# Attention with a routed expert layer: landmark inverse per two batches in two PSUM banks, q, k and v loads issued by ScalarE, and a new order of work

## The chip, the cores and the metric

The kernel runs on one core of a Trainium2 chip. The metric is the device time of one execution in microseconds (us); a kernel is run several times and the median counts. Engines are called PE (matrix products), VectorE (DVE in the profile), ScalarE (ACT), GpSimd (POOL) and SyncE (SP, which only issues DMAs here).

## The reference

Two layers follow each other. The first is a landmark attention over 8 batches x 8 heads, 576 rows of 64 values each; the second sends each of the 4608 rows (512 values) to one of 8 experts.

```
q_lm, k_lm = means of q and k over 18 rows each          # 32 landmarks per head
A  = softmax(q  k_lm^T / 8);  Bm = softmax(q_lm k_lm^T / 8);  C = softmax(q_lm k^T / 8)
Z  = Bm^T / (norm_1(Bm) * norm_inf(Bm) + 1e-6)
for _ in range(6): Z = 2 Z - Z Bm Z                       # approximate inverse of Bm
x  = A Z C v                                              # rows of all heads side by side
e  = argmax(x w_gate);  g = softmax(x w_gate)[e];  s = sigmoid((x w_output_gate)[e])
out = g * s * relu(x w1[e]) w2[e]
```

## The kernel before

Work is cut into 16 groups: a group is 4 heads of one batch, so that 4 x 32 landmarks fill the 128 partitions; two groups are a batch, two batches a pair. For each group q, k and v are loaded into a scratch region (`load`, L211 to L222; the region lies where the weights of the last three experts come later). GpSimd adds up the landmark sums of q and k (`landmark_sums`, L224, five additions each), ScalarE scales them (L239), PE transposes q, k and the landmarks in blocks that ScalarE copies out of PSUM (`transposes`, L243 to L258). PE then makes the scores C and A (L265) and Bm (a block of its own, L280). `softmax_c` (L268) reads C in a column order that the matmul's moving operand gives it, transposes the result (L298) and multiplies it with v (L308). `softmax_a` (L315) is VectorE work apart from one exponential; its result AT stays in SBUF.

`iteration(b)` (L340) serves one batch. With W = Z0 Bm scaled and V = Z0 C v kept side by side (96 columns), each of six steps applies W to both, and VectorE writes 2 cur - W cur (L379). Per step there are 2 groups x 4 heads = 8 matmuls of 32 x 32 x 96, on the four diagonal 32 x 32 tiles of the array, into one PSUM bank (`ps_m`). Column sums come from matmuls with a block of ones (L364). The end transposes V (L386), multiplies it with the gate weights (L397) and writes both masked by head into vbd (L391, L399).

`outputs(b)` (L406) makes five blocks of x per batch, four of 128 rows and one of 64 (L422); ScalarE casts x into a row tile (L426), VectorE adds up the gate logits (L428). `routing` (L448) serves a pair: argmax, place of each row in its expert's list, matmuls for the running counts (L499 to L501), then per block of 128 rows a GpSimd copy that puts row number and coefficient behind the row (L528) and a scatter into a DRAM list sorted by expert (L530).

The expert layer works on tiles of 128 rows of one expert: `fetch` (L670) reads rows and coefficients (SP), `turn_x` transposes them, `up` (L701) multiplies by w1 and ScalarE applies relu, `turn_h` transposes where needed, `down` (L732) multiplies by w2, VectorE scales (L743) and GpSimd scatters the result (L745). Weights are loaded by GpSimd with a cast (L142, L145), four parts per expert, the first experts once the first pair is ranked, the last three after the scratch region is free. Tiles come in stages: 8 and 10 tiles on the two fullest experts after the first pairs, 8 more, and a last stage that needs the last routing (L720 with operand x; here 12 tiles).

Order: each piece of work is a Python generator that issues instructions and yields: L loads, G landmark sums, M landmark scaling, T transposes, C and A the softmaxes, N the inverse, O outputs, R routing, E expert weights, X expert tiles. The string ORDER (L20) says which generator goes on next, so it fixes the order of instructions on every engine's queue; `need` (L187) holds a generator until a mark is set, and "want"/"hold" keep two users of one PSUM tile apart. Each engine runs its queue strictly in the order written, SP's loads included. PSUM has eight banks: `ps_m` 1, `ps_o` 2, `ps_t` 2, `ps_v` 1, and `ps_s` 2, which later serve the expert tiles.

Of the kernel before, what the change touches and what calls it, by code (L numbers as in the profile page):

```python
# [20 lines left out]
    "TTTGTTLTMCTGCTTACGCMCATTCTLMATCCTLAAAAGTCALCMTTCTCNGANLMCNATCGTLALCAACTGMCLTTANTLAMNCCTLGCANCNNLTCAN"  # L21
    "AANMGTCCTNNLTATAOLGAMCCNLGATOAACCTMAGNOCANTLTACTMNTANCLMNONNCACNLACNGOTTCGTMCANOALONTTATLOCCNOATNCGA"
    "AMNOCTRRCTCNARLRMNRTTTRLARCLNTNGCMNRRLGRRCRARAAACTCNCLTRTNLRNTAGOTLMATNRTEENRCRCONRCRNAGCNONTAMAACCG"
    "AEOTXTATNONLXCAALNCMGATTACCOTCAEAEXXOMXCOOLXTNMATXGAOLLRTRTNXERGLAXCXXMTXCNTRGCACRMTECCTAATNRARXMNCC"
    "XNXXNARRLTCENTAXCEXNXLTACTXLGTXARAALNLRGRETXXCNXMTNGCNAAXXONRXETXCNXNXAOLXANAOTNRAXNACOMNCGXTONCEXML"
    "TNALCRTXAGOCCXLXOTXXAMCXCAXGRETOCAOXXRCOTNNTTTXXERNXERCMNXXRRXXANREETXEXCNXRXARCRNXRRAXEMXEXREAETXXT"
    "CTXNXTRNRCTXRNXXXCLXAXEXCCEXXXXCRNCOXCEAAOAXXACXXXXXNEAXXAXXEXNOEXXEONXXNXXEOANRXXXXRXXNXXXRENXNXANE"
    "XXXXAXNXXXNAXXOXOOXOXXXOXRRRRRXRXXXXRXXRXXXXRRXXXRRRXXXXXXXXXRRXXXXXXRXXXXXXXRRXXXXXXXXXXXX"
# [4 lines left out]
def kernel(  # L33
# [14 lines left out]
    m = 32  # L48
# [54 lines left out]
    wg = cpool.tile([D, H, 2 * E], F32, name="wg")  # L103
# [56 lines left out]
    zeros = cpool.tile([128, ROW], I32, name="zeros")  # L160
    nc.vector.memset(zeros, 0)
    nc.vector.memset(zeros[:, HD // 2:HD // 2 + 1], 1 << 20)
# [15 lines left out]
    rows_p = ctx.enter_context(tc.tile_pool(name="rows", bufs=12))  # L178
# [24 lines left out]
    ps_v = ctx.enter_context(tc.tile_pool(name="ps_v", bufs=1, space=PSUM))  # L203
# [7 lines left out]
    def load(k, nm):  # L211
        b, gi = k // NG, k % NG
        src = dict(q=q, k=k_in, v=v)[nm][b, gi * HG:(gi + 1) * HG]
        if nm == "v":
            at = v_places[k % 2]
            t = tail[:CP, at:at + HG * C6 * D].rearrange("p (h x) -> p h x", h=HG)
            nc.sync.dma_start(out=t, in_=src.rearrange("h (p c) d -> p h (c d)", c=C6))
        else:
            at = qk_places[(2 * k + (nm == "k")) % 4]
            t = tail[:, at:at + g * D].rearrange("p (g d) -> p g d", d=D)  # L220
            nc.sync.dma_start(out=t, in_=src.rearrange("h (m g) d -> (h m) g d", g=g))
        groups[k][nm] = t  # L222

    def landmark_sums(k, nm):  # L224
# [4 lines left out]
        nc.gpsimd.tensor_tensor(s, t[:, :hg, :], t[:, hg:, :], op=OP.add)  # L229
        nc.gpsimd.tensor_tensor(s[:, 0:4, :], s[:, 0:4, :], s[:, 4:8, :], op=OP.add)  # L230
        nc.gpsimd.tensor_tensor(s[:, 0:2, :], s[:, 0:2, :], s[:, 2:4, :], op=OP.add)
        nc.gpsimd.tensor_tensor(s[:, 0:1, :], s[:, 0:1, :], s[:, 1:2, :], op=OP.add)
        nc.gpsimd.tensor_tensor(s1, s[:, 0:1, :], s[:, 8:9, :], op=OP.add)
        G["s" + nm] = s1
# [8 lines left out]
    def transposes(k):  # L243

        G = groups[k]
        for nm in ("q", "k"):
            tv = G[nm].rearrange("p (gp par) d -> p gp (par d)", par=2)
            lm = G["l" + nm].rearrange("p a d -> p (a d)")
# [3 lines left out]
            for c0 in range(0, hg + 1, 4):  # L252
                n = min(4, hg + 1 - c0)
                p = ps_t.tile([128, 4, 128], F32, tag="tp", name="tp")
# [5 lines left out]
    def scores(p, lhs, rhs, cols=lambda x: x):  # L260
        for par in range(2):
            pr = slice(64 * par, 64 * par + 64)
            for h in range(HG):
                hs = slice(32 * h, 32 * h + 32)
                nc.tensor.matmul(p[hs, par, :hg * 32], lhsT=lhs[pr, hg, hs], rhs=cols(rhs[pr, :hg, hs]))  # L265
        return p[:, :, :hg * 32]

    def softmax_c(k):  # L268
        G = groups[k]
        b, gi = k // NG, k % NG  # L270
        if gi == 0:
            batches[b]["BC"] = sm.tile([128, NG, 32 + D], F32, tag="BC", name="BC")
        BC = batches[b]["BC"]

        p = ps_s.tile([128, 2, 512], F32, tag="S", name="S")
        sC = scores(p, G["qT"], G["kT"], lambda x: x.rearrange("p (g3 c2) m -> p c2 m g3", g3=CG))
        sC = sC.rearrange("p par (c2 x) -> p par c2 x", x=CP)
        for h in range(HG):
            hs = slice(32 * h, 32 * h + 32)
            nc.tensor.matmul(p[hs, 0, hg * 32:hg * 32 + 32], lhsT=G["qT"][0:64, hg, hs],  # L280
                             rhs=G["kT"][0:64, hg, hs])
        mark("scored C", k)
        nm = sm.tile([128, 1], F32, tag="nm", name="nm")
        nc.vector.tensor_reduce(nm, sC, axis=AX.XYZ, op=OP.max, negate=True)
        yield "hold", "s"
        rc = sm.tile([128, 1], F32, tag="rc", name="rc")
        eC = se.tile([128, g, 32], F32, tag="eC", bufs=1, name="eC")
        nc.scalar.activation(out=eC.rearrange("p g m -> p (g m)").rearrange("p (c2 par x) -> p par c2 x", par=2, x=CP),
                             in_=sC, func=EXP, bias=nm, accum_out=rc)
# [4 lines left out]
        by_chunk = eC.rearrange("p (c x) m -> p c (x m)", c=C6)  # L294
        for c0 in range(0, C6, 3):
            p = ps_t.tile([128, 4, 128], F32, tag="tp", name="tp")
            for c in range(c0, c0 + 3):
                nc.tensor.transpose(p[:CP, c - c0, :], in_=by_chunk[:, c], identity=I128)  # L298
# [3 lines left out]
        yield "want", "v"  # L302
        pv = ps_v.tile([128, 128], F32, tag="pv", name="pv")[:, :D]
# [7 lines left out]
        yield "hold", "v"  # L311
# [3 lines left out]
    def softmax_a(k):  # L315
# [19 lines left out]
        AT = sb.tile([128, g * 32], F32, tag="AT", bufs=6, name="AT")  # L335
        nc.vector.transpose(out=AT, in_=At.rearrange("p a b -> p (a b)"))
        batches[k // NG].setdefault("AT", []).append(AT)
        mark("soft", k)

    def iteration(b):  # L340
        BC = batches[b]["BC"]

        mB = sm.tile([128, NG], F32, tag="mB", name="mB")
# [8 lines left out]


        def apply_w(cur, lo):
            p = ps_m.tile([128, NG, 32 + D + 32], F32, tag="m", name="pw")
            for gi in range(NG):
                for h in range(HG):
                    hs = slice(32 * h, 32 * h + 32)
                    nc.tensor.matmul(p[hs, gi, lo:32 + D], lhsT=cur[hs, gi, :32], rhs=cur[hs, gi, lo:])  # L359
            return p  # L360

        p = apply_w(BC, 0)
        for gi in range(NG):
            nc.tensor.matmul(p[:, gi, 32 + D:], lhsT=blk, rhs=BC[:, gi, :32])  # L364
        ci = sm.tile([128, NG], F32, tag="ci", name="ci")
        nc.vector.tensor_reduce(ci, p[:, :, 32 + D:], axis=AX.X, op=OP.max)
        nc.vector.tensor_scalar(out=ci, in0=ci, scalar1=1e-6, scalar2=None, op0=OP.add)
        nc.vector.reciprocal(ci, ci)
        cur = sm.tile([128, NG, 32 + D], F32, tag="WV", name="WV")
        nc.vector.tensor_tensor(cur, p[:, :, :32 + D], bc(ci, 32 + D), op=OP.mult)  # L370
        yield
        for it in range(6):
            lo = 0 if it < 5 else 32
            p = apply_w(cur, lo)
            if it < 5:
                nxt = sm.tile([128, NG, 32 + D], F32, tag="WV", name="WV")
            else:
                nxt = sm.tile([128, NG, D], F32, tag="V", name="V")
            nc.vector.scalar_tensor_tensor(out=nxt, in0=cur[:, :, lo:], scalar=2.0,  # L379
                                           in1=p[:, :, lo:32 + D], op0=OP.mult, op1=OP.subtract)  # L380
            cur = nxt
            yield

        pt = ps_m.tile([D, NG, 128], F32, tag="m", name="pt")
        for gi in range(NG):
            nc.tensor.transpose(pt[:, gi, :], in_=cur[:, gi, :], identity=I128)  # L386
        VT = sm.tile([D, NG, 128], F32, tag="VT", bufs=1, name="VT")
        nc.scalar.copy(VT, pt)
        vbd = sm.tile([128, NG, 2, VC], F32, tag="vbd", name="vbd")
# [3 lines left out]
        pg = ps_m.tile([128, NG, 2 * E], F32, tag="m", name="pg")  # L393
        for gi in range(NG):
            for h in range(HG):
                hs = slice(32 * h, 32 * h + 32)
                nc.tensor.matmul(pg[hs, gi, :], lhsT=VT[:, gi, hs], rhs=wg[:, gi * HG + h, :])  # L397
        for h2 in range(2):
            nc.scalar.activation(out=vbd[:, :, h2, D:], in_=pg, func=COPY, scale=hm[:, h2:h2 + 1])  # L399
        batches[b]["vbd"] = vbd  # L400
        mark("vbd", b)
        yield

    def outputs(b):

        pair, bb = b // 2, b % 2  # L406
        P = pairs[pair]
        if bb == 0:
            P["L"] = sm.tile([128, CPP, 2 * E], F32, tag="L", name="L")
            P["rows"] = [None] * CPP  # L410
        L, rows = P["L"], P["rows"]
        vbd, ATs = batches[b]["vbd"], batches[b]["AT"]
        for c in range(5):
            t, n, p0 = (4 * bb + c, 128, 0) if c < 4 else (8, 64, 64 * bb)
            ps = slice(p0, p0 + n)
            if rows[t] is None:
                rows[t] = rows_p.tile([128, ROW], I32, tag="row", name="row")
            po = ps_o.tile([128, 2, 512], F32, tag="o", name="po")
            for gi in range(NG):
                for hp in range(2):  # L420
                    hs = slice(64 * hp, 64 * hp + 64)
                    nc.tensor.matmul(po[ps, hp, gi * 2 * VC:(gi + 1) * 2 * VC],  # L422
                                     lhsT=ATs[gi][hs, 128 * c:128 * c + n],
# [584 lines left out]
```

## Time and profile before

| | |
|---|---|
| median of 3 runs | 379.78 us (378.74 to 384.86) |
| profiled execution | 376.81 us |
| its span, first to last instruction | 375.2 us |
| mean granted PE clock | 0.985 of full speed |
| DMA traffic | 66.76 MB, 178 GB/s over the span |
| largest groups | L737 PE 73.9 us, L256 PE 51.2, L257 ScalarE 47.9, L229 GpSimd 43.0 |

How to read it: a row of a group view names line, engine, operation, output <- input and count, then the busy time in us and the mean ns of one, then the engine's idle time just before, and what ended it. A row of waits says who waited for whom: us in total, times, longest. A row of a timeline has the start, the length, and in brackets the idle time before. Rows of busy time by stretch give each engine's busy us, then granted clock, DMA share and GB/s. An fp32 matmul leaves two records.

### The profile page before, as it was taken

How to read it: one execution, taken by the hardware profiler on the slowest of the kernel's cores; microseconds unless marked ns; L12 is line 12 of the kernel's file. 1: busy time of each engine (PE TensorE's matmuls, PEld its weight loads, DVE VectorE, ACT ScalarE, POOL GpSimd, SP SyncE). 2: the span in 40 equal slices, each digit the busy share in tenths (PEclk: the TensorE clock that was granted, in tenths of full speed). 3: DMA queues.
4: the chain of work that ended last, by engine and by line, in shares of the span. 5: the costliest groups of instructions: out<-in, count | busy, mean ns of one | idle time of the engine just before them, and what ended most of it. 6: DMA issues, size and time to landing. Idle time of an engine off the chain costs nothing. (4 is left out here: it accounts for less than half of the span.)

```text
span 375.2 us, 11946 instructions
## 1 busy us (share of the span) xinstructions
PE 323.5 (86%) x4532; PEld 208.1 (55%) x4532; DVE 221.2 (59%) x584; ACT 175.0 (47%) x413; POOL 215.5 (57%) x319
## 2 busy tenths in 40 slices
PE   2888879888888877999998899999979997899992
PEld 1555456565655645676666477666645553455551
DVE  6277677477977384777658672665635674223322
ACT  2676475766737553554555354543234331232320
POOL 3788855644887487278888465784420585122322
PEclk9999899999989998999999999999999999999999
DMA  8866555245637997895587799999992357354221
GB/s 254 268 192 207 176 190 168 71 145 190 184 145 139 293 261 156 216 236 202 116 243 190 146 243 255 228 229 247 228 259 89 117 180 172 64 91 121 73 86 50
DMA packets 46743, 66.76 MB, mean 178 GB/s; under 512 B 16208, under 2 KB 35024, under 8 KB 46672
## 3 DMA queue, kind: packets, MB, share of 16 engines
q0 software_dynamic: 17568, 31.24, 37.4%
q1 hardware_dynamic: 29104, 34.63, 31.9%
q8 instruction: 39, 0.64, 0.7%
q14 instruction: 32, 0.26, 0.3%
HBM read 65.35 MB, written 16.23 MB: 217 GB/s over the span
## 5 line engine op out<-in xcount | busy, mean ns | idle before, releaser
L745 POOL DMA_INDIRECT out_dram<-y,ic x38 | 39.1, 1030 | 88.1 <-DVE y L743 69.9
L737 PE MATMUL py<-W,hT 128*128 (+1 forms) x304 | 73.9, 382 | 6.9 <-DMA W<-in_moe_w_dram 4.0
L743 DVE TENSOR_SCALAR y<-py,ic 128x512 f32<-128x512 f32 x38 | 28.4, 749 | 60.2 <-PE py L737 59.9
L257 ACT COPY W<-tp 128x512 f32<-128x512 f32 (+1 forms) x96 | 47.9, 515 | 31.9 <-PE tp L256 31.6
L256 PE MATMUL tp<-ident,W 128*128 128x128 f32 x288 | 51.2, 298 | 13.3 <-ACT W L257 7.8
L229 POOL TENSOR_TENSOR lms<-W 128x576 f32<-128x576 f32 x30 | 43.0, 1435 | 31.6 <-DMA W<-in_q_dram 30.6
L737 PEld LDWEIGHTS <-hT 128*128 128x128 bf16 x304 | 29.1, 99 | 39.1 <-issue 6.6
L723 ACT ACTIVATE h<-ph 128x512 bf16<-128x512 f32 x40 | 23.9, 597 | 56.0 <-PE ph L720 51.2
L256 PEld LDWEIGHTS tp<-ident,W 128*128 128x128 f32 x288 | 34.5, 148 | 24.5 <-ACT W L257 12.3
L530 POOL DMA_INDIRECT x_sorted<-row,r_slot x36 | 36.7, 1020 | 13.5 <-POOL row L528 8.8
L709 PE MATMUL ph<-xT,W 128*128 128x128 bf16 x576 | 37.7, 219 | 1.5 <-DMA W<-in_moe_w_dram 0.7
L422 PE MATMUL po<-vbd,AT 64*128 64x160 f32 (+1 forms) x320 | 32.8, 324 | 4.4 <-DVE L L428 3.4
L709 PEld LDWEIGHTS <-W 128*128 128x128 bf16 x576 | 33.2, 98 | 4.8 <-issue 2.6
L428 DVE TENSOR_REDUCE L<-po 128x16 f32<-128x128 f32 (+1 forms) x40 | 11.6, 290 | 40.2 <-ACT row L426 40.2
L712 ACT ACTIVATE hT<-ph 128x512 bf16<-128x512 f32 x36 | 21.4, 597 | 27.8 <-PE ph L709 27.6
L426 ACT CAST row<-po 128x512 bf16<-128x512 f32 (+1 forms) x40 | 23.4, 585 | 21.1 <-PE po L422 17.6
L265 PE MATMUL S<-W 64*32 64x288 f32 x512 | 26.1, 466 | 5.7 <-ACT BC L290 4.1
L359 PE MATMUL pw<-WV 32*32 32x96 f32 (+1 forms) x768 | 25.6, 249 | 5.6 <-DVE WV L379 3.4
L422 PEld LDWEIGHTS po<-vbd,AT 64*128 64x128 f32 (+1 forms) x320 | 22.5, 178 | 11.8 <-DVE L L428 5.7
L230 POOL TENSOR_TENSOR lms<-lms 128x256 f32<-128x256 f32 x30 | 24.9, 830 | 2.4
L359 PEld LDWEIGHTS pw<-WV 32*32 32x32 f32 x768 | 15.5, 107 | 16.0 <-DVE WV L379 7.4
L720 PE MATMUL ph<-W,x 128*128 x96 | 22.7, 379 | 1.7 <-DMA out_dram<-y,ic 1.3
(166 smaller groups left out, 530.0 us busy)
## 6 DMA issues: line engine op xcount, KB each, us to landing
W<-in_moe_w_dram POOLq DMA_DIRECT2D x32, 512.0 KB, 11.2
W<-in_q_dram SPq DMA_DIRECT2D x16, 576.0 KB, 6.6
W<-in_k_dram SPq DMA_DIRECT2D x16, 576.0 KB, 6.7
W<-in_v_dram SPq DMA_DIRECT2D x16, 576.0 KB, 5.2
x<-x_sorted SPq DMA_DIRECT2D x26, 128.0 KB, 6.4
x_sorted<-zeros SPq DMA_DIRECT2D x9, 136.0 KB, 1.9
ic<-x_sorted SPq DMA_DIRECT2D x38, 1.0 KB, 5.5
out_dram<-y,ic POOLq DMA_INDIRECT x38, 2.9
```

The lines of the kernel that those rows point to most:

```text
L229: nc.gpsimd.tensor_tensor(s, t[:, :hg, :], t[:, hg:, :], op=OP.add)
L230: nc.gpsimd.tensor_tensor(s[:, 0:4, :], s[:, 0:4, :], s[:, 4:8, :], op=OP.add)
L256: nc.tensor.transpose(p[:, i, :], in_=tv[:, c0 + i] if c0 + i < hg else lm, identity=I128)
L257: nc.scalar.copy(tT[:, c0:c0 + n, :], p[:, :n, :])
L265: nc.tensor.matmul(p[hs, par, :hg * 32], lhsT=lhs[pr, hg, hs], rhs=cols(rhs[pr, :hg, hs]))
L359: nc.tensor.matmul(p[hs, gi, lo:32 + D], lhsT=cur[hs, gi, :32], rhs=cur[hs, gi, lo:])
L422: nc.tensor.matmul(po[ps, hp, gi * 2 * VC:(gi + 1) * 2 * VC], lhsT=ATs[gi][hs, 128 * c:128 * c + n], rhs=vbd[hs, gi].rearrange("p a b -> p ...
L530: i = nc.gpsimd.indirect_dma_start(out=xs, out_offset=bass.IndirectOffsetOnAxis(ap=slot[:, c:c + 1], axis=0), in_=rows[c], in_offset=None)
L709: nc.tensor.matmul(ph[:, 128 * i:128 * i + 128], lhsT=columns(t, dc * F + (half * FCH // 2 + i) * 128, 128), rhs=t["xT"][:, dc, :], start= ...
L737: nc.tensor.matmul(t["py"], lhsT=t["hT"][:, fc, :], rhs=columns(t, DCH * F + fc * HD, HD), start=(fc == 0), stop=(fc == FCH - 1))
L743: nc.vector.tensor_scalar(out=y, in0=t["py"], scalar1=t["coef"], scalar2=None, op0=OP.mult)
L745: i = nc.gpsimd.indirect_dma_start(out=out, out_offset=bass.IndirectOffsetOnAxis(ap=t["id"], axis=0), in_=y, in_offset=None, bounds_check= ...
```

## The change

- The inverse serves a pair (four groups) at once. The tile has two PSUM banks, one for each batch. The second batch's heads move between neighbouring tiles (head h sits in the partitions of h or of h^1, in turn), so that its matmuls run on off-diagonal tiles. VectorE writes S = 2I - W (a new function `complement`), which is the stationary operand, ScalarE copies the new W and V. Column sums take two matmuls per pair (one with a swapped block of ones). V is transposed for two groups in one go, and the gate weights lie block-wise on 128 partitions with zeros between, so one matmul per head and batch serves both groups.
- `scores` appends Bm as a tenth block of columns to C's first half; the column order that C needs is made by ScalarE when it applies the exponential. AT is written as 512 + 64 columns (AT, AU).
- `outputs` serves a pair: eight blocks of 128 rows and one that holds the two 64-row rests.
- From group 2 on, ScalarE issues the q, k and v loads. Group 0's landmark sums are the five additions, on VectorE.
- `ps_v` is gone: pv and the routing counts use `ps_t`. The routing writes one row block at a time; its coefficient is a VectorE reciprocal straight into the row tile, the row number a GpSimd copy made one block ahead. The end-of-list markers are copied from DRAM to DRAM.
- ORDER is a new string (another order of the same generators); y has three buffers instead of four.

```diff
-    def load(k, nm):
+    def load(k, nm, eng):
...
-            nc.sync.dma_start(out=t, in_=src.rearrange("h (m g) d -> (h m) g d", g=g))
+            eng.dma_start(out=t, in_=src.rearrange("h (m g) d -> (h m) g d", g=g))
...
-                load(k, nm)
+                load(k, nm, nc.scalar)
...
-    def scores(p, lhs, rhs, cols=lambda x: x):
+    def scores(p, lhs, rhs, more=0):
...
+            n = hg + more * (1 - par)
...
-                nc.tensor.matmul(p[hs, par, :hg * 32], lhsT=lhs[pr, hg, hs], rhs=cols(rhs[pr, :hg, hs]))
+                nc.tensor.matmul(p[hs, par, :n * 32], lhsT=lhs[pr, hg, hs], rhs=rhs[pr, :n, hs])
...
-        pv = ps_v.tile([128, 128], F32, tag="pv", name="pv")[:, :D]
+        pv = ps_t.tile([128, 512], F32, tag="tp", name="pv")[:, :D]
...
+        def apply_w(p, lhs, rhs, lo, swaps, swap):
             for gi in range(NG):
+                for bb in range(2):
+                    for h in range(HG):
+                        at = h ^ (bb & swaps)
+                        to = at ^ (bb & swap)
+                        hs, os = slice(32 * at, 32 * at + 32), slice(32 * to, 32 * to + 32)
+                        nc.tensor.matmul(p[os, NG * bb + gi, lo:32 + D], lhsT=lhs[hs, NG * bb + gi], rhs=rhs[hs, NG * bb + gi, lo:])
+
+        def complement(S, W):
+            nc.vector.scalar_tensor_tensor(out=S, in0=W, scalar=-1.0, in1=twice, op0=OP.mult, op1=OP.add)
...
         for it in range(6):
             lo = 0 if it < 5 else 32
-            p = apply_w(cur, lo)
+            p = banks()
+            apply_w(p, S, cur, lo, (it + 1) % 2, it < 5)
             if it < 5:
...
+                complement(S, p[:, :, :32])
+                nc.scalar.copy(cur, p[:, :, :32 + D])
             else:
...
-            nc.vector.scalar_tensor_tensor(out=nxt, in0=cur[:, :, lo:], scalar=2.0,
-                                           in1=p[:, :, lo:32 + D], op0=OP.mult, op1=OP.subtract)
...
+                nc.scalar.copy(cur, p[:, :, 32:32 + D])
...
+        for t in range(CPP):
+            if t == ROWS - CPP and pair >= 1:
+                yield from need("routed", pair - 1)
...
+        name_row(0)
         for c in range(CPP):
-            if c % 2 == 0:
-                yield
-            nc.gpsimd.tensor_copy(rows[c][:, HD // 2:].rearrange("p (n x) -> p n x", x=2),
-                                  idc[:, c, None, :].to_broadcast([128, META // 2, 2]))
+            yield
+            nc.vector.reciprocal(rows[c][:, HD // 2:HD // 2 + 1].bitcast(F32), co[:, c:c + 1])
             i = nc.gpsimd.indirect_dma_start(
...
+            if c + 1 < CPP:
+                name_row(c + 1)
```

More of the change, by code (lines that the diff above doesn't have):

```diff
@@ L407, in outputs @@
         P = pairs[pair]
[L408 to L417, printed above, removed]
-            po = ps_o.tile([128, 2, 512], F32, tag="o", name="po")
[L419 to L423, printed above, removed]
-                                     rhs=vbd[hs, gi].rearrange("p a b -> p (a b)"))
-            pv = po[ps, :, :NG * 2 * VC].rearrange("p t (gh e) -> p t gh e", e=VC)
-            nc.scalar.copy(rows[t].bitcast(BF16)[ps, :HD].rearrange("p (t gh d) -> p t gh d", t=2, d=D),
+        L = P["L"] = sm.tile([128, CPP, 2 * E], F32, tag="L", name="L")
@@ L806, in softening_a @@
             if k >= 6:
-                yield from need("out", (k - 6) // NG)
+                yield from need("half" if (k - 6) % (2 * NG) < NG else "out", (k - 6) // (2 * NG))
             yield from softmax_a(k)
```

264 lines of the change are left out of this document (148 added, 116 removed).

## The prediction, made before the changed kernel had run

> **What bounds the kernel now.** I read the page's busy line first, then the busy time by stretch, then the waits of PE, POOL and SP, and last the timelines around the places that the change touches.
>
> ```profile
> PE 323.5 (86%) x4532; PEld 208.1 (55%) x4532; DVE 221.2 (59%) x584; ACT 175.0 (47%) x413; POOL 215.5 (57%) x319
> ```
> ```profile
> core 0: us, PE busy (x) PEld busy (x) DVE busy (x) ACT busy (x) POOL busy (x), PEclk, DMA share, GB/s
> 20.00:105.00 85.00, 71.60 (x1385) 47.91 (x1385) 62.65 (x163) 54.55 (x146) 57.89 (x87) 0.98 0.56 176
> 105.00:150.00 45.00, 34.98 (x567) 24.06 (x560) 28.14 (x74) 24.03 (x59) 33.30 (x48) 0.92 0.81 191
> 150.00:290.00 140.00, 132.05 (x2001) 90.34 (x2001) 86.11 (x245) 65.97 (x153) 82.26 (x113) 1.00 0.93 210
> ```
> PE is the busiest engine everywhere. From 150 to 290 us it idles 8.0 of 140 us: work taken off PE there shortens the time one for one. From 20 to 105 us it idles 13.4 of 85 us and from 105 to 150 us 10.0 of 45 us, so other things share the limit. The waits say which:
>
> ```profile
> PE tp L256 <- ACT W L257: 7.8, 11, 2.9
> PE py L737 <- DMA W<-in_moe_w_dram: 4.0, 1, 4.0
> PE pw L359 <- DVE WV L379: 3.4, 8, 0.7
> ```
> ```profile
> POOL lms L229 <- DMA W<-in_q_dram: 30.6, 8, 6.5
> ```
> ```profile
> SPq L221 <- PE tp L256: 26.2, 11, 8.1
> ```
> PE waits for many short ScalarE copies and once, for 4.0 us, for weights. POOL waits 30.6 us for q and k loads, which feed its landmark sums and then PE. SP holds q and k loads back, 26.2 us in all, until PE has transposed the old tile, so they are just in time.
>
> **PE work that the change removes.** Start-to-start times of PE's timeline give the price of each block:
>
> ```profile
> 150.71 0.53 PE L359 MATMUL pw<-WV 32*32 32x96 f32 x16
> 151.17 0.21 PE L499 MATMUL pr<-r_ohb,neg_lower_bf 128*128 128x72 bf16 x1
> ```
> ```profile
> 162.08 0.71 PE L265 MATMUL S<-W 64*32 64x288 f32 x16
> 162.73 0.88 PE L308 MATMUL pv<-W 96*32 96x64 f32 x48
> 163.54 0.66 PE L256 MATMUL tp<-ident,W 128*128 128x128 f32 x4
> ```
> ```profile
> 167.87 0.32 PE L397 MATMUL pg<-wg,VT 64*32 64x16 f32 x16
> 168.12 0.40 PE L697 MATMUL pt<-ident_bf,x 128*128 128x128 bf16 x4
> ```
> ```profile
> 193.16 0.89 PE L265 MATMUL S<-W 64*32 64x288 f32 x16
> 193.83 0.25 PE L280 MATMUL S<-W 64*32 64x32 f32 x8
> 194.01 0.40 PE L697 MATMUL pt<-ident_bf,x 128*128 128x128 bf16 x4
> ```
> ```profile
> 205.72 0.76 PE L422 MATMUL po<-vbd,AT 64*64 64x160 f32 x8
> 206.41 0.33 PE L256 MATMUL tp<-ident,W 128*128 128x128 f32 x1
> ```
> ```profile
> 210.64 0.63 PE L364 MATMUL pw<-BC,blk_ones 128*128 128x32 f32 x4
> 211.11 1.03 PE L737 MATMUL py<-W,hT 128*128 128x512 bf16 x4
> ```
> ```profile
> L386 PE MATMUL pt<-ident,V 128*64 128x128 f32 x16 | 3.3, 294 | 0.4 <-DVE V L379 0.4
> ```
> Inverse steps. One step of one batch is 16 records in 0.46 us (150.71 to 151.17): four 32x32 tiles of the array, four records of 96 columns each, 1.2 ns per column and tile. After it, a step serves two batches: 32 records on eight tiles, in two banks. The nearest row is the A score, also eight tiles in two banks: two records of 288 columns per tile in 0.65 us (162.08 to 162.73), 1.13 ns per column and tile. Eight tiles run as fast each as four do, so the pair's step should again cost about 0.46; I take 0.50. Its bounds: 0.39 (16 records of L397 take 0.25, 8 of L280 take 0.18, so 9 ns per further record) and 0.92 (the second bank takes turns). Six full steps save 0.42 each, the last, narrower one is taken at 0.3: 4 pairs x (6 x 0.42 + 0.3) = 11.3 us.
>
> The Trainium skill, TensorEngine Tiling (Array Packing), section Performance Considerations, gives every matmul an overhead of about 60 cycles whatever its width; at the 2.4 GHz that the Trainium skill's TensorE: Matmul & The Clock Gate gives in Part 1, that is an estimated 25 ns, so 32 records would need 0.80 us and the two-bank step would save next to nothing. The trace disagrees: 48 records of L308 start within 0.81 us, 17 ns each.
>
> C scores: 0.67 + 0.18 us (193.16, 193.83, 194.01) become one block as in A, with 32 columns more for half of it, 0.69: 16 x 0.16 = 2.6 us. Column sums (L364): 0.47 per batch, about 0.5 per pair: 4 x 0.44 = 1.8. Transposes of V (L386): 3.3 us busy, partly under other work, half as many: 1.2. Gate products (L397), 0.25 per batch, once per pair with 128 rows: 1.0. The 64-row output block (L422), 0.69 per batch, both halves of a pair together on four tiles instead of two: 2.8, nothing if they take turns. Sum 20.7 us; bounds 6.6 (no overlap in L359 and L422) and 23.3 (steps at 0.39).
>
> **What comes back or is added.** ScalarE and VectorE:
>
> ```profile
> L257 ACT COPY W<-tp 128x512 f32<-128x512 f32 (+1 forms) x96 | 47.9, 515 | 31.9 <-PE tp L256 31.6
> L299 ACT COPY W<-tp 96x384 f32<-96x384 f32 x32 | 15.0, 475 | 9.7 <-PE tp L298 9.2
> L379 DVE SCALAR_TENSOR_TENSOR WV<-WV,pw 128x192 f32<-128x192 f32 x40 | 13.7, 342 | 6.3 <-PE pw L359 6.1
> L379 DVE SCALAR_TENSOR_TENSOR V<-WV,pw 128x128 f32<-128x128 f32 x8 | 2.3, 285 | 3.7 <-PE pw L359 3.7
> L292 DVE RECIPROCAL rc<-rc 128x1 f32<-128x1 f32 x16 | 2.3, 141 | 0.0
> L221 SPq DMA_DIRECT2D W<-in_q_dram x16: 328/431/1474, 0.9 to 189.1; - x16
> ```
> A step ended with one VectorE operation of 0.342 us; now VectorE makes 2I-W (0.285) while ScalarE copies 384 columns (0.475 by L299), so a step's latency grows by 0.13 us, but there are half as many. I leave the 3.4 us of PE waits there as they are: bounds 1.7 and 6. ScalarE gains 24 copies (24 x 0.475, some 11 us) and loses half of several small ones, which I don't count. It also issues 42 loads: SP needs 0.328 to 1.474 us for one (median 0.431), so 42 x 0.43 = 18 us, and up to 1.5 us at once in front of a copy. From 20 to 105 us ScalarE would be busy about 54.6 + 12 + 4 = 71 of 85 us. It stays under PE, but PE's largest wait is for its copies: I take +2 us; bounds 0 and 18. VectorE gains 36 reciprocals (5.1 us) and its two L379 groups (16 us) become 24 x 0.285 = 6.8; with 221 of 375 us busy it hides both. POOL loses four small copies; its 36 row copies stay. The four small gate-weight loads instead of two are used tens of us later. SP is emptied of loads; x fetches behind them get free, which I price at nothing, since PE shows no wait for x before 300 us.
>
> Loads. The q, k and v bytes are the same. The Trainium skill, DMA: Bandwidth & Descriptors, section Issuing engines are not separate DMA queues, says that a second issuing engine saves only issue time; no run here shows it yet, and I count no faster landing. In ScalarE's stream the loads of a group stand behind copies, so they are issued rather later than now. In the stretch to 105 us, which holds some 40% of the saved PE work (8 us), I therefore give half back: +4 (bounds 0 and 8, and the slower rival).
>
> Weights. Now the four parts of the first expert go out over 18 us, with POOL's sums and their waits between them:
>
> ```profile
> 115.57 1.53 POOL L142 DMA_DIRECT2D W<-in_moe_w_dram  x2 [1.25 <-issue]
> ...
> 133.92 0.76 POOL L145 DMA_DIRECT2D W<-in_moe_w_dram  x1 [0.25 <-issue]
> ```
> In the new order three parts go in a row and the fourth after one sum: the 4.0 us wait of L737 goes, -4 (bounds 0 and -5). At the start group 0's sums become trees and ScalarE copies sooner: -1.
>
> Tail. The last routing must end before the last stage's rows can be fetched; tiles of the stage before cover it:
>
> ```profile
> 289.46 0.17 PE L501 MATMUL pr<-r_cb,ones_bf 128*128 128x8 bf16 x1
> 319.77 1.89 PE L720 MATMUL ph<-W,x 128*128 x8 [1.34 <-DMA out_dram<-y,ic]
> ```
> ```profile
> 296.79 0.99 POOL L530 DMA_INDIRECT x_sorted<-row,r_slot  x1 [0.67 <-DVE xT L699]
> 310.04 0.99 POOL L530 DMA_INDIRECT x_sorted<-row,r_slot  x1 [0.28 <-POOL row L528]
> ```
> ```profile
> 312.60 1.32 SPq L680 DMA_TRANSPOSE x<-x_sorted  x1
> ```
> From L501 to the last scatter's end are 21.4 us now, to the fetch 23, to usable rows some 27; PE has about 26.5 us of tiles behind L501. In the new order L501 stands 1.5 tiles later, so only about 19 us of tiles are left. The chain starts sooner (slots computed at once, 7 us now to the first scatter) but the nine scatters are strung between three output scatters, two weight parts and reciprocals that wait behind VectorE's tile work: 9 x 1.0 + 3 x 1.0 + 2 x 0.8 + copies and their waits of 3 = 17, after 2.5; fetch and landing 6: 25 to 26. PE is short of 6 where it now is short of 2: +4 (bounds 0 and 8).
>
> Sum: 375.2 - 20.7 + 2 + 4 - 4 - 1 + 4 = 359.5 us of span. The profiled execution took 376.81, 1.6 over its span: 361.1. The median of the runs is 379.78, 3.0 above the profiled one: 364.1.
>
> **Rivals.** The second bank takes turns. The price is 11.3 + 2.8 us, so 378. For it: eight diagonal and off-diagonal tiles of 32 rows are in no row here. The overhead per matmul in the Trainium skill's TensorEngine Tiling (Array Packing), above, would end here too. Against it: the per-tile rates of L265 and L359 above. Chance 0.20.
>
> Slower: the load chain becomes the limit. A load of q or k, then POOL's sums, a ScalarE scale, PE's transposes, and only then the next load into that place; POOL's 30.6 us of waits show that it is tight. If each of 14 groups has its loads issued behind three copies that SP didn't wait for (3 x 0.515 + 0.33 = 1.9 us), the chain grows by 14 x 1.9 = 26 us: 390. It cancels the gain from 1.1 us per group and is slower by 2% from 1.65. Against it: SP already waited for PE's transposes (26.2 us), and these copies follow the same transposes. Chance 0.13.
>
> Faster still: the new order also fills half of the 23.4 us that PE idles from 20 to 150 us, instead of giving work back there: 364.1 - 12 = 352. For it: the half number of steps and the freed SP; against it: ScalarE is fuller and the two transpose banks now also serve pv and pr. Chance 0.14.
>
> **How the numbers follow.** My forecast has 0.50, its own range is 357 to 371; 0.03 is left for anything else. The time is that of the likeliest, 364. From 350 to 381 lie all but the slower rival, the lowest part of the fast one and the rest: 0.20 left out. A measurement of this kernel tells about 2% (7.6 us) from no change. Faster by that, below 372.2: 0.50 + 0.14 and a little of the turns rival, 0.66. Within: the turns rival mostly, 0.20. Slower: 0.14.
>
> **What would show it.** Right: the profile shows steps of 32 records of pw in about 0.5 us, C scores at 0.7 us without a second block, PE busy near 303 us, no 4 us wait of L737's successor, and the DMA bytes as before. Wrong: pw steps at 0.9 us; POOL's wait for q loads well over 30 us or PE's for ScalarE copies well over 10 us; a gap of 6 us or more before the last stage. If PE busy falls as worked out and the time does not, the load chain is to blame.

## The result, and the profile after

The changed kernel takes 410.56 us (median of 4, 406.48 to 412.25), the one before 379.26 on the same chip: ratio 1.084, 95% interval 1.078 to 1.089. The forecast was 364. Now and then an execution comes out over 1.5% slower than the fastest of its kernel; ratios leave such runs out, medians do not, so differences below go by the ratios. The profiled execution took 412.25 us, its span is 410.6.

The page's busy line and its row of the granted clock, kernel after:

```profile
PE 330.1 (80%) x4286; PEld 208.8 (51%) x4316; DVE 208.6 (51%) x582; ACT 181.8 (44%) x413; POOL 211.7 (52%) x315
PEclk9976768979758689899789769999999998999999
```

The same three stretches as before the change (us, busy time of each engine, clock, DMA share, GB/s):

```profile
20.00:105.00 85.00, 63.95 (x1032) 39.85 (x1032) 44.07 (x92) 46.10 (x116) 43.17 (x64) 0.78 0.42 127
105.00:150.00 45.00, 32.37 (x542) 21.26 (x543) 29.08 (x93) 20.87 (x54) 31.60 (x48) 0.70 0.75 185
150.00:290.00 140.00, 123.31 (x1857) 87.83 (x1872) 78.24 (x232) 69.28 (x156) 82.74 (x117) 0.91 0.78 185
```

In the first stretch every engine does less in the same 85 us (VectorE 44.1 instead of 62.7, DMA 127 instead of 176 GB/s): all are kept waiting. Over the whole span PE has less matrix work than before, but the granted clock fell from 0.985 to 0.886 (0.78 in this stretch), so its busy time does not show it. The span grew by 35.4 us: 6.6 of them PE busy (330.1 - 323.5), 28.8 PE idle. These two are rough, since the trace lacks 30 records of PE (4286 products against 4316 weight loads).

Who waited, after:

```profile
POOL lms L238 <- DMA W<-in_q_dram: 56.0, 9, 13.1
POOL lms L238 <- DMA W<-in_k_dram: 16.5, 4, 6.6
PE tp L266 <- DMA W<-in_q_dram: 12.0, 3, 6.1
PE ph L745 <- DVE wb L670: 3.5, 1, 3.5
PE ph L745 <- DMA x<-x_sorted: 3.3, 1, 3.3
```

GpSimd waits 72.5 us for q and k where it waited 30.6 for q (no wait for k stands in the list before). The place to see why is ScalarE's timeline (its own work, and ACTq, the loads that it issues), 31 us after the start:

```profile
31.36 0.31 ACT L319 ACTIVATE BC<-pv,rc 128x64 f32<-128x64 f32 x1 [0.66 <-PE pv L316]
31.36 0.34 ACTq L226 DMA_DIRECT2D W<-in_v_dram  x1
31.74 0.37 ACT L267 COPY W<-tp 128x256 f32<-128x256 f32 x1
31.77 0.47 ACTq L230 DMA_DIRECT2D W<-in_q_dram  x1
32.27 0.44 ACTq L230 DMA_DIRECT2D W<-in_k_dram  x1
38.87 0.59 ACT L267 COPY W<-tp 128x512 f32<-128x512 f32 x1 [6.75 <-DMA W<-in_k_dram]
```

and the same three loads in SP's queue, first in the kernel before, then in e1 below, which is the changed kernel with SyncE as issuer:

```profile
18.85 0.33 SPq L217 DMA_DIRECT2D W<-in_v_dram  x1
19.27 1.47 SPq L221 DMA_DIRECT2D W<-in_q_dram  x1
20.84 0.37 SPq L221 DMA_DIRECT2D W<-in_k_dram  x1
```
```profile
23.12 0.33 SPq L226 DMA_DIRECT2D W<-in_v_dram  x1
23.55 1.38 SPq L230 DMA_DIRECT2D W<-in_q_dram  x1
25.01 0.38 SPq L230 DMA_DIRECT2D W<-in_k_dram  x1
```

They are v of group 2 and q and k of group 3. From 23 us on their place is free, as e1 shows; ScalarE comes to them at 31.4, after a dozen instructions of its own, 8.2 us later than SyncE and 12.5 later than before. Then it stands still for 6.75 us, and PE for 6.09, until they have landed:

```profile
37.75 1.09 PE L266 MATMUL tp<-ident,W 128*128 128x128 f32 x4 [6.09 <-DMA W<-in_q_dram]
```

### The profile page after: what moved, and what is told of

Same layout as the page of the kernel before. It is cut to its first block, busy times and chain, and to the rows that moved or that the text cites. A ratio compares the mean times of both kernels' runs of the same rounds, so it can differ in the third digit from the quotient of the medians.

```text
span 410.6 us, 11490 instructions
## 1 busy us (share of the span) xinstructions
PE 330.1 (80%) x4286; PEld 208.8 (51%) x4316; DVE 208.6 (51%) x582; ACT 181.8 (44%) x413; POOL 211.7 (52%) x315
## 3 DMA queue, kind: packets, MB, share of 16 engines
q0 software_dynamic: 17568, 31.24, 35.4%
## 4 chain that ended last, share of the span: by engine, by line
PE 39%; DMA 23%; DVE 12%; POOL 8%; issue 8%; ACT 7%; POOLq 1%; ACTq 1%; SPq 0%; DVEq 0%
DMA out_dram<-y,ic 8%; PE py L762 8%; DMA W<-in_q_dram 6%; PE tp L266 6%; PE ph L734 5%; PE po L447 5%; DMA x<-x_sorted 4%; PE S L276 3%; DMA x_sorted<-row,r_slot 3%; PE pw L376 3%; PE ph L745 2%; PE tp L305 2%; PE pv L316 2%; POOL lms L238 2%; ACT row L450 2%
## 5 line engine op out<-in xcount | busy, mean ns | idle before, releaser
L238 POOL TENSOR_TENSOR lms<-W 128x576 f32<-128x576 f32 x30 | 42.4, 1412 | 73.1 <-DMA W<-in_q_dram 56.0
L762 PE MATMUL py<-W,hT 128*128 (+1 forms) x280 | 70.7, 379 | 3.9 <-DVE hT L755 2.2
L266 PE MATMUL tp<-ident,W 128*128 128x128 f32 x288 | 59.0, 336 | 17.7 <-DMA W<-in_q_dram 12.0
L266 PEld LDWEIGHTS tp<-ident,W 128*128 128x128 f32 x288 | 40.7, 170 | 36.9 <-issue 13.8
L452 DVE TENSOR_REDUCE L<-po 128x16 f32<-128x128 f32 x36 | 10.5, 291 | 55.7 <-ACT row L450 55.7
L447 PE MATMUL po<-vbd,AT 64*128 64x160 f32 x256 | 30.1, 360 | 9.1 <-DVE L L452 8.2
L276 PE MATMUL S<-W 64*32 64x288 f32 (+1 forms) x512 | 30.3, 538 | 2.0 <-ACT W L267 2.0
L737 ACT ACTIVATE hT<-ph 128x512 bf16<-128x512 f32 x36 | 21.5, 598 | 23.4 <-PE ph L734 22.6
L450 ACT CAST row<-po 128x512 bf16<-128x512 f32 x36 | 21.1, 586 | 23.1 <-PE po L447 17.9
L447 PEld LDWEIGHTS po<-vbd,AT 64*128 64x128 f32 x256 | 21.6, 215 | 17.7 <-DVE L L452 13.9
L305 PE MATMUL tp<-ident,eC 128*96 128x128 f32 x96 | 19.3, 326 | 9.6 <-ACT eC L295 5.2
L376 PE MATMUL pw<-WV,SI 32*32 32x96 f32 (+1 forms) x768 | 16.4, 277 | 9.6 <-ACT WV L402 5.5
```

The lines of the kernel that those rows point to most:

```text
L238: eng.tensor_tensor(s, t[:, :hg, :], t[:, hg:, :], op=OP.add)
L266: nc.tensor.transpose(p[:, i, :], in_=tv[:, c0 + i] if c0 + i < hg else lm, identity=I128)
L276: nc.tensor.matmul(p[hs, par, :n * 32], lhsT=lhs[pr, hg, hs], rhs=rhs[pr, :n, hs])
L376: nc.tensor.matmul(p[os, NG * bb + gi, lo:32 + D], lhsT=lhs[hs, NG * bb + gi], rhs=rhs[hs, NG * bb + gi, lo:])
L450: nc.scalar.copy(rows[t].bitcast(BF16)[:, :HD].rearrange("p (t gh d) -> p t gh d", t=2, d=D), pv[:, :, :, :D])
L762: nc.tensor.matmul(t["py"], lhsT=t["hT"][:, fc, :], rhs=columns(t, DCH * F + fc * HD, HD), start=(fc == 0), stop=(fc == FCH - 1))
```

## The experiments

Ratios are to the kernel before, timed beside each set on the same chip. It took 379 us there, except for e5 to e8 (another chip, 399.6) and e9 to e12 (402.6): across sets only ratios are compared. On those two chips PE also stands still where no wait is shown ("issue" is 13% of the chain that ended last in e8, 9% in e4), so what they show need not hold to the microsecond on the first chip.

### Who issues the loads, and where

e1, after with SyncE as issuer at the same places; e2, before with ScalarE as issuer:

```
e1:  -                load(k, nm, nc.scalar)        e2:  -                load(k, nm)
     +                load(k, nm, nc.sync)               +                load(k, nm, nc.scalar)
```

> The changed kernel, but SyncE issues the q, k and v loads again, at the same places of the order. Load theory (the loads stand too late in ScalarE's queue, GpSimd's sums and PE wait for them, and PE's clock falls while it idles): 365 to 380 us, GpSimd's waits for q and k loads back from 72 to under 40 us, PE clock at least 0.96. Order theory (the new order and the pair-wise inverse themselves make PE wait, whoever issues the loads): 400 us or more, waits for loads as before.

Measured 383.04 us, ratio 1.008 (1.002 to 1.014): some 29 us of the loss are gone. The expectation was a little too good: 365 to 380 us, a clock of at least 0.96 (0.95 came) and under 40 us of GpSimd's waits for q and k, where the profile has 46.3:

```profile
POOL lms L238 <- DMA W<-in_q_dram: 34.8, 6, 10.6
POOL lms L238 <- DMA W<-in_k_dram: 11.5, 1, 11.5
```

> The kernel before, with one part of the change alone: ScalarE issues the loads from group 2 on, at the old places of the order. Load theory: slower, 390 to 410 us, GpSimd waits 45 us or more for loads, clock down to 0.9 to 0.95. Order theory: 378 to 385 us, since the old order is kept.

Measured 398.17 us, ratio 1.046 (1.039 to 1.054): in the old kernel, with nothing else changed, ScalarE's loads cost some 18 us. ScalarE's timeline of e2, and GpSimd's just before:

```profile
44.61 0.31 ACT L240 ACTIVATE lm<-lm 128x128 f32<-128x128 f32 x1 [3.50 <-POOL lm L234]
44.62 0.33 ACTq L222 DMA_DIRECT2D W<-in_q_dram  x1
```
```profile
41.06 1.40 POOL L230 TENSOR_TENSOR lms<-W 128x576 f32<-128x576 f32 x1 [2.67 <-DMA W<-in_q_dram]
```

The kernel before issues this load (group 5's q) at 36.39 us; here it stands behind an activation that waits for GpSimd's sums, 8.2 us later. The sums in turn had waited 2.67 us for an earlier load of the same queue: the queue closes a ring. The other side shows in PE's waits of e2 (before, 7.8 us for the same copies, longest 2.9, and 4.1 for the scores):

```profile
PE tp L257 <- ACT W L258: 16.0, 13, 4.7
PE S L266 <- ACT BC L291: 7.8, 4, 4.4
```

e3 and e4: every load as early in the program as its marks allow; e3 by ScalarE, e4 by SyncE.

```
     for c in ORDER:
         advance(c)
+        advance("L")
```

> The changed kernel, ScalarE still issues the loads, but each is put into the program as soon as the old tile has been used, instead of at its place in the order string. Load theory: most of the loss returns, 370 to 385 us. If it is ScalarE as issuer as such that costs (issue time in front of copies), not the place: 395 us or more. Order theory: 400 or more.

> The changed kernel, loads issued by SyncE and put into the program as soon as the old tile has been used. Load theory: the fastest of these four, 358 to 372 us. Order theory: 400 or more.

Measured: e3 398.86 us (1.048, 1.040 to 1.056), e4 381.13 (1.004, 0.999 to 1.010). So by the ratios the place in the order is worth some 14 us with ScalarE (1.084 to 1.048) and the issuer some 16 more (to 1.004); with SyncE the place is worth nothing that is clear of noise (e1 1.008, e4 1.004). Both expectations missed: e3 was to end below 385, e4 below 372. The first says that ScalarE is a bad issuer even where the loads stand as early as their marks allow; the second that something else eats the saved PE work. The rest is about that. The page's busy line and clock of e4:

```profile
PE 314.1 (83%) x4286; PEld 199.7 (53%) x4316; DVE 210.9 (56%) x582; ACT 181.0 (48%) x413; POOL 213.6 (56%) x315
PEclk9969969998657699999999999999989998999999
```

### Is the work saved, and what is a microsecond of PE worth?

e7 leaves both batches on the same tiles of the array:

```
-        apply_w(p, BC[:, :, :32], BC, 0, 0, 1)
-        for bb, ones in enumerate((blk, swapped)):
-            apply_w(p, S, cur, lo, (it + 1) % 2, it < 5)
+        apply_w(p, BC[:, :, :32], BC, 0, 0, 0)
+        for bb, ones in enumerate((blk, blk)):
+            apply_w(p, S, cur, lo, 0, 0)
```

> e4 with the second batch's heads left on the same four diagonal tiles of the array as the first's (no swap; both halves still in two banks, the result is the reference's). It prices the forecast's largest term. If eight tiles are what makes the pair's step as short as one batch's was, a step of 32 records grows from 0.50 to about 0.92 us and the time by some 11 us to 392 (the group of inverse matmuls from about 19 to about 30 us busy). If the tiles don't matter and records just follow each other, both stay: 381.

A step in e4, then in e7 (the next row's start ends it):

```profile
188.12 0.56 PE L376 MATMUL pw<-WV,SI 32*32 32x96 f32 x32
188.61 0.71 PE L276 MATMUL S<-W 64*32 64x288 f32 x16
```
```profile
194.72 0.86 PE L376 MATMUL pw<-WV,SI 32*32 32x96 f32 x32
195.52 0.71 PE L276 MATMUL S<-W 64*32 64x288 f32 x16
```

0.49 against 0.80 us: eight tiles do what the forecast said, and its rival of turns (0.92) has no case. But the time, 400.51 us, has ratio 1.003 (0.998 to 1.008), like e4's and that of e8 on the same chip (1.004): 7 us of the inverse's products came back (25.8 us of PE against 19.1 in e4) and cost nothing that shows.

e9 and e10 issue every product of the inverse twice, e13 and e14 leave two products per expert tile out:

```
e9:   +            for _ in range(2):            # around the 8 products of a step
e10:  -                for bb in range(2):
      +                for bb in [0, 1] * 2:
e13, e14:
-            if part is None or fc // (FCH // 2) == part:
+            if part is None or (fc // (FCH // 2) == part and fc not in (1, 6)):
```

> The kernel before with every product of the inverse (L359) issued twice; the second writes the same values into the same place, so the output is the reference's. PE gets about 8 x (6 x 0.46 + 0.3) = 24 us more work, spread from 30 to 290 us. It prices a microsecond of PE work in the old kernel, which the forecast took as one for one from 150 to 290 us and as half before. Forecast's view: 18 to 24 us longer, ratio to before 1.047 to 1.063. Rival, other things (loads, GpSimd, VectorE) set the pace and PE's work hides between them: under 8 us, ratio below 1.02.

> e4 with every product of the pair's inverse issued twice (same values, output as the reference's): about 4 x (6 x 0.5 + 0.3) = 13 us more PE work. If PE is as much the limit in the changed kernel as the forecast took it to be: 10 to 13 us longer than e4, ratio to before 1.03 to 1.04. Rival, the new order leaves PE waiting for other engines wherever the inverse stands, so that its work is hidden: ratio to before 1.00 to 1.015, as e7 (8 us more PE work, 1.0028) suggests.

> The kernel before, with two of the eight products per tile left out of the second expert matmul (L737) in the 26 tiles ahead of the last stage: 26 x 2 x 0.257 = 13.4 us less PE work from 140 to 315 us and nothing else changed (it leaves out a quarter of that sum over hidden units). It prices a microsecond taken off PE in the stretch for which the forecast said one for one. Forecast's view: 11 to 13.4 us faster, ratio 0.965 to 0.972. Rival, other chains set the pace: under 5 us, ratio 0.987 or more. From e9 (28 us more busy cost 15) I expect half or less.

> e4 with the same two products per tile left out (same part of the result missing): 13.4 us less PE work in the changed kernel. If PE is what limits it there: ratio to before 0.97 to 0.975 against e4's 1.0044. If its waits for other engines and transfers are the limit: 0.99 to 1.005.

| | PE busy of the products changed | ratio | in us |
|---|---|---|---|
| e9 (before, more) | inverse, 29.9 to 51.8: +21.9 | 1.038 (1.025 to 1.050) | +15.1 (10 to 20) |
| e10 (e4, more) | inverse, 19.1 to 37.3: +18.2 | 1.054 (1.041 to 1.067), e4 1.004, e11 1.011 | +17 (from e11, same chip) to +20 |
| e13 (before, less) | L737, 73.9 to 62.4: -11.5 | 0.990 (0.978 to 1.002) | -3.9 (-8.4 to +0.7) |
| e14 (e4, less) | the same 52 products | 1.001 (0.996 to 1.007), e4 1.004 | -1.2 |

The bases of e9 and e10 were profiled on another chip, so the group of the products is compared and not PE's total. Doubling the inverse's products costs seven tenths of the added time, or all of it; taking products out of the expert tiles gives back a third or less. It is not the same work: the doubled products lengthen every step of the inverse, while those left out lie in tiles that fill the gaps between steps. And e7's 7 us cost nothing. So a microsecond of PE has no one price here. Where the saving went in e14, by PE's timeline (last count, then the first product of the last stage):

```profile
289.61 0.17 PE L525 MATMUL pr<-r_cb,ones_bf 128*128 128x8 bf16 x1
...
306.01 1.89 PE L745 MATMUL ph<-W,xT 128*128 x8 [3.67 <-DVE ge L671]
319.37 3.15 PE L745 MATMUL ph<-W,x 128*128 x7 [7.19 <-DMA x<-x_sorted]
```

The count stands 5.8 us earlier than in e4 (295.38), and PE then waits 10.9 us instead of 6.9 for the last table and rows; the first tile behind it runs at half the clock.

### The clock

Four stretches of e4:

```profile
88.00:92.00 4.00, 1.10 (x31) 0.37 (x19) 3.83 (x15) 1.21 (x4) 0.88 (x4) 0.90 0.71 183
92.00:96.00 4.00, 2.93 (x38) 1.62 (x41) 3.81 (x18) 2.12 (x7) 1.54 (x3) 0.50 0.72 275
...
112.00:116.00 4.00, 3.36 (x78) 2.33 (x86) 3.05 (x10) 2.27 (x8) 2.44 (x6) 0.50 0.02 4
116.00:120.00 4.00, 3.84 (x103) 2.32 (x93) 3.38 (x8) 1.75 (x4) 3.92 (x5) 0.69 0.65 90
```

PE waits 2.6 us for the routing's sums, and the clock is at half for most of the next 24 us. Over 90 to 120 us, before and then e4:

```profile
90.00:120.00 30.00, 25.76 (x488) 17.27 (x488) 23.65 (x74) 17.82 (x48) 22.96 (x34) 0.94 0.56 167
```
```profile
90.00:120.00 30.00, 21.50 (x386) 14.30 (x387) 24.27 (x81) 12.32 (x32) 21.73 (x32) 0.60 0.56 171
```

e5 fills that gap, e6 four gaps:

```
+    def fill(n):
+        p = ps_t.tile([128, 4, 128], F32, tag="tp", name="fill")
+        for i in range(n):
+            nc.tensor.matmul(p[:, i % 4, :], lhsT=I128, rhs=I128)
...
+        if pair == 0:
+            fill(20)
```

> e4 with 20 idle products (identity by identity, 128 x 128 fp32, into a spare PSUM tile that nobody reads, about 3.3 us of PE) put right ahead of pair 0's running-count matmuls, where PE stood still for 2.6 us in e4. The output is the reference's. Clock theory: in e4 the granted clock fell to 0.50 right behind that gap (92 to 96 us) and stayed at 0.50 to 0.75 until 116 us, so the 20 us of gain was lost to the clock more than to idling; with PE kept busy the clock behind it stays near 1.00 and the time falls by 5 to 8 us to 373 to 376. Rival, the waits themselves are the loss and the clock follows something else: clock at 92 to 116 us stays near 0.6 and the time is 380 to 384.

> e4 with idle products at four places where it had gaps of over 1 us before 150 us and a low clock behind them: 6 in group 0's softmax, 8 ahead of the first inverse matmuls of pairs 0 and 1, 24 ahead of pair 0's counts, 14 ahead of the first expert tile (60 x 0.165 us, some 10 us of PE work). The output is the reference's. Clock theory: no stretch from 20 to 150 us under 0.9, time 366 to 373 although PE does 10 us more. Rival (waits, not the clock): 381 to 388.

The stretch from 90 to 120 us in e8, which has no filling and ran on the same chip, and then in e5:

```profile
90.00:120.00 30.00, 21.16 (x385) 13.41 (x385) 22.44 (x81) 11.98 (x32) 21.74 (x32) 0.66 0.59 174
```
```profile
90.00:120.00 30.00, 20.23 (x373) 14.49 (x372) 21.95 (x83) 11.55 (x30) 19.73 (x30) 0.77 0.53 162
```

The clock rose from 0.66 to 0.77, but the groups behind this stretch come no earlier for it: the transpose of the same group's landmarks, in e8 and then in e5,

```profile
158.81 0.27 PE L266 MATMUL tp<-ident,lm 128*128 128x128 f32 x1
```
```profile
159.80 0.27 PE L271 MATMUL tp<-ident,lm 128*128 128x128 f32 x1
```

So other waits set the pace there. The times: e5 398.66 us, 0.996 (0.991 to 1.001), short of the 5 to 8 us expected but 0.8% under e8, with intervals that just overlap; e6 403.77, 1.011 (1.000 to 1.022), with 0.83 in this stretch and some 10 us more PE work. No run kept the clock full, so a few us may still lie in it; the bulk of the gain was not found there.

### Sums, last routing, order of the tiles, transfers

e11 lets GpSimd's sums go on after each R, e12 adds e5's filling (16 products); e8 issues the last routing's rows and table without gaps:

```
e11:  +        if c == "R":                     e8:  +        if ("counted", NPAIR - 1) in marks:
      +            advance("G")                      +            advance("R")
```

> e4 with GpSimd's landmark sums allowed on after each letter of the routing, so that group 9's q sums stand behind three row scatters of pair 0 instead of seven. In e4 these sums began at 104.5 us (in the kernel before at 92.3), though their load had been issued at 88.6; group 9 was turned at 104 us (before 100), group 12 at 160 (before 151). If the scatter chain in front of the sums is what costs those 9 us: 373 to 377 by the chip of e4, ratio to before 0.985 to 0.995. Rival, the rest of the stretch (half clock behind PE's gap, VectorE) sets the pace: ratio 1.000 to 1.008 as e4.

> e11 with 16 idle products ahead of pair 0's counts, as in e5 (output as the reference's): both mends of the stretch from 87 to 125 us at once. If both the clock and the sums hold it up: ratio to before 0.97 to 0.985, the first version that beats both kernels. If either is only a follower of the other or of a third thing: 0.99 to 1.00, no better than e5.

> e4 with the last routing's remaining pieces (nine scatters, then the last table) each issued one letter of the order earlier, without gaps of several letters. In e4 the scatters end at 315.9 us, the table at 314.4, and PE stands still 3.4 us for the table and 3.5 us for the last stage's rows. If that chain is what the tail costs (the forecast's +4), both waits fall under 1 us each and the time falls by 4 to 6 us to 375 to 377. Rival: VectorE's table work and the scatters then delay the tiles' own copies and output scatters by as much: 380 to 383.

e11 402.43 us, 1.011 (1.000 to 1.022): group 9 is turned no earlier (106 us, 104 in e4) and GpSimd's wait for q is 56.9 us where e4's is 42.4, so the sums only wait in another place. e12 401.52, 1.012 (0.998 to 1.026), where 0.985 or less was expected if both causes added up. e8 400.26, 1.004 (0.999 to 1.009): its scatters end 16.5 us after the last count instead of 20.5, but the first fetch comes as late as before (24.3 against 24.8).

e15 and e16 leave out the late weights:

```
-                load_expert(r, part, e)
+                if r < EARLY:
+                    load_expert(r, part, e)
+                else:
...
+                    nc.gpsimd.memset(W[:, r, layer, t * NG * F:(t + 1) * NG * F].bitcast(I32), 0)
```

> The kernel before without the weight loads of the three last experts: GpSimd writes zeros in their place, so these experts' rows come out as zeros; 12.6 of 66.8 MB are not moved, nearly all from 210 to 290 us, where the DMA share was 1.0 to 1.2. If transfers set the pace there: 10 us or more faster, ratio under 0.975. If PE does (it is 95% busy there): no change, 0.99 to 1.00.

> e4 without the same weight loads (same rows zero). If the transfers of 240 to 310 us are where the changed kernel's saved PE work is lost: 10 us or more faster than e4, ratio to before under 0.98. If not: 0.995 to 1.005 as e4.

379.27 us, 1.003 (0.998 to 1.008), and 379.02, 1.004 (0.999 to 1.008): nothing, though 12.6 MB less are read (52.8 against 65.4 MB in the old kernel) and the DMA share at 150 to 290 us falls from 0.93 to 0.68 there. These transfers don't set the pace.

e17 gives the end of the order from group 15 on a new form, e18 adds e5's filling:

```
+    for c, event, n in (("N", ("vbd", NPAIR - 1), 2), ("O", ("out", NPAIR - 1), 1), ("R", ("counted", NPAIR - 1), 1),
+                        ("R", ("routed", NPAIR - 1), 1)):
+        advance("A")
+        while event not in marks:
+            if advance(c):
+                tiles(n)
...
```

> e4 with another end of the order, from group 15's softmax on: two tile pieces between the inverse steps, one between the outputs, the last count issued as soon as the outputs are through, so that it stands 1.5 tiles (some 6 us of PE) earlier in PE's queue and these tiles behind it; all the same work. Tail theory (the last count plus a fixed chain of some 30 us sets the end; the 8 us that PE idles in it in e4 are the lost gain): the count comes 5 to 6 us earlier, PE's idle time between it and the last stage falls from 8 to about 2 us, the time by 5 to 6 us, ratio to before 0.985 to 0.992. Rival, the count waits as long as before for PE, ScalarE and VectorE (the steps' latency is no longer covered) or the chain grows by the tiles put into it: 1.00 to 1.01.

> e17 with e5's 20 idle products ahead of pair 0's counts. If both add up: ratio to before about 0.977 to 0.987, under e17 by 0.005 to 0.008. If the idle products do nothing, as e12 suggests: the same as e17.

390.25 us, 1.028 (1.020 to 1.036), and 389.27, 1.029 (1.021 to 1.036): slower. The count came at 298.3 us, 3 later than in e4, although fewer tiles stand ahead of it: PE idles more between the last steps and outputs, and its clock falls (250 to 290 us, e4 and then e17):

```profile
250.00:290.00 40.00, 34.27 (x476) 21.32 (x481) 17.88 (x59) 16.09 (x31) 14.89 (x17) 0.96 1.06 203
```
```profile
250.00:290.00 40.00, 30.46 (x408) 17.88 (x408) 15.70 (x51) 11.99 (x26) 14.99 (x18) 0.83 1.18 231
```

It also ends the theory of a fixed chain: rows could be fetched 18.9 us after the count (24.8 in e4). No version that does all the work beat the kernel before clear of noise.

## Why the prediction was wrong, point by point

**Loads: the step that failed first.** The forecast took +4 us, "rather later than now", with bounds 0 and 8; e1 shows some 29. Of the 46 us by which the forecast was off, some 25 are this term; the other 21 or so have the size of the saved PE work (20.7), which e1 and e4 do not turn into time. The mechanism was among the rivals: the load chain as the limit, priced at 26 us and given a chance of 0.13. Its ground against, that these copies follow the same transposes that SP waited for, was wrong: e2's q load stood behind an activation that waits for GpSimd. SP's 26.2 us of waiting were free because from 18 to 100 us that queue holds loads alone. They were also not all of its waits: the v loads, which stand in the same queue ahead of the next q and k, waited longer still over the whole kernel:

```profile
SPq L217 <- PE pv L308: 76.3, 7, 22.1
SPq L217 <- PE tp L256: 32.4, 4, 9.1
```

The Trainium skill, DMA: Bandwidth & Descriptors, section Issuing engines are not separate DMA queues, says that a second issuer saves only issue time. In the rows above an issue took 0.33 to 0.47 us in ScalarE's queue and 0.33 to 1.47 in SyncE's; the loss from the issuer's own work ahead of the load is not in that rule, and it decided.

**PE work.** The sizes held: 0.49 us for a step (0.50 forecast), and in after's timeline

```profile
255.17 0.74 PE L276 MATMUL S<-W 64*32 64x320 f32 x16
255.85 1.04 PE L762 MATMUL py<-W,hT 128*128 128x512 bf16 x4
...
280.99 0.43 PE L384 MATMUL pw<-BC,blk_ones 128*128 128x64 f32 x2
281.26 0.39 PE L384 MATMUL pw<-BC,blk_swapped 128*128 128x64 f32 x2
281.49 1.03 PE L762 MATMUL py<-W,hT 128*128 128x512 bf16 x4
```

0.68 us for the C scores with Bm (0.69) and 0.50 for a pair's column sums (0.5). So the second bank does not take turns, and 32 records do not cost 0.80 us. The ground for the last was misread in the forecast, though: it set 25 ns against records, and every fp32 product leaves two of them. The step's 16 products take 31 ns each and the 24 of L308 took 34, so neither row speaks against 25 ns a product.

**One for one: the step that failed second.** "Work taken off PE there shortens the time one for one" was read from PE being 94% busy. e13 took 11.5 us of it out of the old kernel, mostly in that stretch, and got 3.9 back (at most 8.4); e14 got 1.2 in the changed one. The busy share did not say what removing work is worth. e4, whose loads SyncE issues as early as their marks allow, stands at the old time. By the busy lines its span of 379.4 is before's 375.2, less 9.4 of PE busy time (the clock was lower, 0.931 against 0.985, and 30 records are missing, so this is rough), plus 13.6 of PE idle time.

**ScalarE, +2.** In e4 PE waits 5.4 us for the WV copies and 6.9 for the softmax C (3.4 for VectorE's WV and 2.5 for that softmax before): 6.4 more; for the copies of the transposes it waits 4.8 instead of 7.8. The net of 3.4 is within the bounds.

**Weights, -4.** The wait of L737's successor for weights is gone from the list. **Tail, +4.** PE waits 3.5 us for the table and 3.3 for x, where before it waited 0.6 for the table and 1.9 for the rows: +4.3, as forecast. What these two are worth in time is not shown: e8 and e17 could not cash the tail in.

**What would show it.** The text named POOL's wait for q well over 30 us, and the load chain as the one to blame: 56.0 us, and it was.

**Open.** Which chain paces the old kernel and e4 from 90 us on is not settled. Shown is what does not by itself: the sums' place, the late weights, the last routing, the clock behind one gap. That the waits replace each other, as in e14, is seen in one trace and not proven for all. No run separates the new order from the pair-wise work, so it stays open whether the saving is lost to the order or would be lost in any order; that the order can cost as much is seen in e17.

## What to carry to other kernels

Let a transfer that waits for a free place be issued by an engine that has nothing else to do; on an engine with work, price the waits ahead of it in its queue and the work behind it, not the 0.3 us of issue. Before counting a saving one for one, take that much work out of the old kernel, wherever it can be left out: one run would have shown that 11.5 us of PE in the expert tiles are worth about 4 (at most 8.4). When a change has several parts, forecast the part that touches a ring of waits by the ring, not by a share of a gain.

## What the runs showed of the hardware

- One PE gap of 2.6 us was followed by half the clock for most of 24 us, with PE 57 to 84% busy in that time (by stretches of 4 us); it rose to 0.69 in the stretch in which PE was 96% busy, and was full in the next. The Trainium skill, TensorE: Matmul & The Clock Gate, Part 1, has the clock fall after an idle window of about 3.4 us and come back after one busy window; here the fall came sooner (0.59 over the microsecond in which the gap ended), and the return waited for a stretch in which PE was busy nearly all the time.
- Four off-diagonal and four diagonal 32 x 32 tiles, each set in a bank of its own, run side by side: 32 records in 0.49 us, against 0.80 on the same four tiles.
- The same kernel (before) took 379 us on one chip and 400 and 403 on two others.
